# One core, three layers: the list that orders all operations and names their engines, made anew

## The chip, the cores and the metric

The kernel runs on one core of one Trainium2 chip. The core has TensorE (matmuls, PE in the rows), VectorE (DVE), ScalarE (ACT), GpSimd (POOL) and SyncE (SP), which here issues all transfers. Each engine works through its own queue in order; engines wait for each other by semaphores. The metric is the device time of one execution in microseconds (us), the median of the runs shown.

## What is computed

The reference chains three layers over 2 sequences of 768 tokens: a retention attention with 8 heads of 64 (blocks of 64 tokens, a decaying state of 64 x 64 for each head), a channel mix of width 512 with a hidden layer of 1024, and a gated convolution of five taps between two products of 512 x 512.

```python
intra = np.einsum('bhic,bhjc->bhij', qb, kb) * Dmask[None]
intra = np.einsum('bhij,bhjd->bhid', intra, vb)
inter = np.einsum('bhid,bhde->bhie', qb * lam_pow[None], kv_state)
out[:, :, sl] = intra + inter
...
xk = mu_k * x + (1.0 - mu_k) * x_prev
xr = mu_r * x + (1.0 - mu_r) * x_prev
k = np.maximum(xk @ w_k, 0.0)
v = k * k @ w_v
r = 1.0 / (1.0 + np.exp(-(xr @ w_r)))
x = (r * v)
...
gate_pre += conv_w[k][None, None, :] * xp[:, k:k + S, :]
gate = 1.0 / (1.0 + np.exp(-gate_pre))
return gate * (x @ w_val) @ w_out
```

`w_k`, `w_v`, `w_r`, `w_val`, `w_out` and `conv_w` come as float64; the kernel turns them into float32 itself, by work on their two 32-bit words.

## The kernel before

The program is a set of named operations, each of one or a few instructions, with a list of engines that may run it. A string, `ORDER`, lists all names in the order in which they are emitted, with a letter behind a colon where an operation may run on more than one engine (V VectorE, A ScalarE, G GpSimd); without a letter the first engine allowed is taken. `emit` walks the string. Each engine's queue is thus the string's operations of that engine, in the string's order; nothing else moves them. A name may stand only behind all that it depends on.

```python
    def emit(token):
        name, _, e = token.partition(":")
        o = ops[name]
        o.engine = e or o.engines[0]
        assert o.engine in o.engines and name not in emitted, token
        assert emitted.issuperset(o.deps), (token, o.deps - emitted)
        ...
        o.fn(of_letter[o.engine])
```

The names that the text uses, with their lines:

- *Weights* (`conversion`, L326 to L346), for each of 28 pieces of 128 x 512 that come from HBM: `a`, `b` on ScalarE; `c` (L331), `d`, `e` (L337), `f` (L340) on VectorE, `c` and `f` on GpSimd also; then the split of the float32 into a high part `h` (ScalarE) and a low part `l` (L346, VectorE or GpSimd). Every product is made of three matmuls, high by high, high by low and low by high, so that each operand, weights and activations alike, has a high and a low part.
- *Attention*, twelve chunks c of 128 tokens: transposes `Tk`, `Tq` on TensorE and their copies `Ek`, `Eq`; query times decay powers `Q` (L488); key times decay `D` (L497); scores `S` (L513), their product with the mask `M` (L520, VectorE, scores in PSUM); state products `U` (L534); state times decay `O` (L553) and the sum `N` (L556); output `Y`, `Z` (L595), copied to SBUF by `X` (L622, L624).
- *Channel mix*, six groups g of 256 tokens: `mk`, `mr` are the two mixes: a scaling `a0`, `a1` (L647, L649; any of three engines), a scaled sum `b0`, `b1` (L652, VectorE), the high part `h` and the low part `l` (L632). `r` is the sigmoid branch, `k` the hidden layer (relu `e`, square into the high part `h`, square again `q` (L749, L751), low part `l` (L757)), `v` the product back and its multiplication with r (L767), into tile `big` (`x2`).
- *Gated convolution*, for each g and each half m: the gate `g` in two pieces, a first tap as a scaling (L801, L803) and four more taps as scaled sums (L799, VectorE alone), then a sigmoid (L808); the split of x2 `s` (L777, L779); the value product `a` with its multiplication by the gate (L818) and its split (L632); the last projection `p` (L836), its copy (L843, L844) and the output transfer.
- `warm0` to `warm23` (L903): products of the identity that no one reads; ten of them stand at the end.

TensorE's products land in four PSUM tiles that are used in turn, the activations in rings of 26 tiles of 512 and 8 of 1024 floats, and the raw weights of the last layer in a ring of three.

Of the kernel before, what the change touches and what calls it, by code (L numbers as in the profile page):

```python
# [27 lines left out]
    Eq3:A w3f:G w1 Y2 N2.1 Z2 U3 S3 Q3 w0h mr0.0h mr0.0l:G w0l:G mr0.1a1:A q4 O3.0:V N3.0 X2:A
    M3 mr0.1b1 mr0.1b0 w3h w1a Tk4 Ek4:A w1c:V D4:G O3.1:G w1d v4 w3l:V mr0.1h w1e Y3 Z3 X3:A
    r0.1.0 mk0.0b1 Tq4 mk1.0a0:A r0.0.0 N3.1 mk0.1a1:V mk1.1a1:G w1b mr1.0a0:A mr1.1a0:A  # L30
    mr1.0a1:A mk1.0b0 Eq4:A w1f:V w1h k5 mr1.0b0 mk0.1b1 Tk5 mr1.0b1 mr1.1b0 mr1.1a1:A mr1.1b1
    mr0.1l:G w1l:G U4 mr1.0h w6 S4 Ek5:A O4.0:V w6a r0.1.1 mr1.0l:V mr1.1h x0 w6b r0.0.1 r0.0s
    r1.0.0 r0.1s mk1.0a1:G mk0.0a0:V jk3.1 w6c:V w6d w4 mk0.0b0 w7 mr1.1l:G w6e mk1.0b1 N4.0
    r1.0.1 w6f:G O4.1:V N4.1 r1.1.0 v5 mk0.0h mk1.1a0:G M4 D5:G w4a w4c:V q5 Tq5 w4d mk0.0l:G
    w7a Q4 w4e mk0.1a0:A mk0.1b0 w6h w6l:G w7c:V w4b w4f:V r1.1.1 Y4 w7d U5 mk1.0h Z4 H2 w7b
    w5 w5a w5c:V w5d Eq5:A w5b mk1.1b0 w4h jq3.2 mk1.0l:G w4l:G r1.1s S5 k0.1.0 r1.0s w9
    k1.1.0 w10 w10a mk0.1h w7e w5e w8 w7f:V w8a Q5 w8b w7h w10c:V k0.0.0 w9a mk1.1b1 mk1.1h
    jq3.3 jq3.0 w9b w5f:G w16 w16b w10d w5h w7l:V mk0.1l:G k1.0.0 mk1.1l:G w8c:V w8d w8e
    k0.1.1 w9c:V k1.1.1 w9d jk3.3 w8f:V w11 w5l:G w16a jq3.1 w9e w12 w11a k1.0.1 w11c:V jk3.0
    k7 M5 w8h w11b w8l:V k1.0e:A w9f:G O5.0:G w9h k1.1e:A w9l:G w10b k0.1e:A w11d w12a k0.0.1  # L40
    w12c:G w17 N5.0 w10e jk3.2 w10f:V X4:A k0.2.0 k1.1h k1.2.0 k1.2.1 k0.0e:A Bq3 w11e w11f:G
    k6 v6 Bk3 w12b w10h w10l:G k0.2.1 w15 D6:V Y5 jq4.1 Q6:G k1.0h k1.0q:A w13 S6 w16c:V w17a
    U6 w11h w11l:G Z5 jq4.0 w12d k0.3.0 k1.3.0 X5:A v7 w16d k1.3.1 w16e w16f:V w16h D7:G
    k1.0l:V jq4.2 w17b M6 w17c:V k0.0h N6.0:V O6.1:G w12e w12f:G w17d w16l:G N6.1 k0.3.1 w13a
    U7 k0.1h k0.2e:A k1.2e:A Q7:G w17e w17f:V k0.0q:A mr2.0a0:G v8 Y6 w12h S7 k0.1q:G k0.1l:G
    Z6 k0.0l:V w15a w14 w17h w12l:V v0.1.0 w17l:V v1.0.0 w15c:V jq4.3 k1.1q:A k1.1l:V w13c:V
    mk2.0a0:A w13b w14a k0.3e:A v1.1.0 k0.2h w13d w13e v1.1.1 k1.3e:A M7 w15d O7.0:G w14c:V
    w13f:V w13h w13l:G w15e v0.0.0 w14d jk4.3 w15b mk2.0b0 k8 w14b w18 w15f:V mk2.0a1:A N7.0
    D8:G k0.2q:A mk2.1a1:V mk2.0b1 mk2.1b1 v0.1.1 v1.0.1 O7.1:G w15h X6:V N7.1 w14e w14f:V
    k1.2h Y7 U8 k0.2l:G k1.3h w18a w14h w15l:V mr2.1a0:A Z7 w14l:V k11 jk4.1 k1.3q:A w18c:V  # L50
    w18d w18e w18b w18f:V H3 mk2.1a0:A k0.3h v0.0.1 mk2.1b0 k1.2q:G jk4.0 k1.2l:G v0.0.2
    v1.0.2 k0.3q:A k1.3l:G v1.0.3 k0.3l:V v0.0.3 w18h jk4.2 cw0 mk2.0h X7:A Bq4 v1.0e mk2.0l:G
    mk2.1h k2.0.0 mk2.1l:V k2.0.1 v9 Bk4 v0.0e S8 k9 k2.1.0 Q9:G k2.1.1 w19 w19a jk5.1 O8.0:G
    jk5.0 M8 k2.0e:V k2.3.0 w18l:G mk3.0a0:A k2.3.1 mk3.1a1:G mk3.1b1 mk3.0a1:V w19b D11:G
    k2.1e:V N8.0 mr3.0a0:G mr3.0b0 cw cwa D9:G cwb mr3.0a1:V Q8:V O8.1:G Y8 N8.1 mr2.0a1:A S9
    mk3.1a0:G mk3.1b0 mk3.0b0 Z8 U9 k2.3e:A O9.0:V N9.0 v0.1.2 jq5.0 k2.0h mr2.1b0 k2.2.0
    k2.0q:V jq5.1 k2.2.1 mk3.0b1 mk3.0h jk5.3 jq5.3 w19c:V w19d w19e w19f:V k2.2e:V w19h
    mr2.0b1 M9 v10 mk3.0l:G k3.1.0 k3.3.0 cwc:V w19l:G v1.1.2 jk5.2 v1.1.3 H4 mk3.1h mk3.1l:G
    mr2.1a1:V mr2.1b1 mr2.1h cwd k3.3.1 k10 k2.0l:V k3.1.1 X8:A mr2.1l:G mr2.0b0 mr2.0h Y9
    k2.1h O9.1:V Bk5 D10:V N9.1 jq5.2 Bq5 U10 k2.3h k2.3q:A k2.3l:V S10 Z9 X9:V v1.1e  # L60
    mk4.0a1:A s0.0h v0.1.3 M10 Q10:V v0.1e mr2.0l:G mk4.1a1:V mk4.1b1 k2.2h k2.2q:A O10.0:V
    cwe cwf:V k3.2.0 k3.2.1 N10.0 mr3.1a1:A O10.1:V v11 mk4.1a0:A mk4.1b0 k2.2l:G N10.1
    k3.2e:A mk4.1h cwg r2.0.0 mr4.1a1:G cwt r2.0.1 k3.1e:V k3.1h S11 Y10 mk4.0a0:V Q11:G
    mr3.1a0:G U11 g0.1.10:A Z10 O11.0:V X10:A r2.1.0 r2.0s mk4.0b0 r2.1.1 k2.1q:A H5 mr4.0a1:G
    M11 N11.0 Y11 Z11 k3.0.0 g1.1.10:V k3.1q:G k3.1l:V v2.0.0 r2.1s mr3.1b1 x1 mr4.0a0:A
    mr4.1a0:G k2.1l:G mr4.1b0 mr4.0b0 k3.3e:A X11:A mr5.1a1:V mk5.1a1:V mr3.1b0 mr3.0b1 v2.1.0
    mr4.0b1 mr3.0h v2.0.1 mk4.1l:G k3.2h mr5.0a1:A v2.0.2 v2.0.3 mk5.0a1:V mk4.0b1 k3.2q:G
    mk4.0h v2.0e s2.0h mk4.0l:G g2.0.00:A mk5.1a0:V k4.2.0 k4.2.1 mk5.1b1 mk5.1b0 mk5.1h
    k4.2e:V k4.3.0 k3.0.1 k3.0e:A k3.0h k3.0q:G k3.0l:V k4.1.0 k4.1.1 k4.1e:V g2.0.10:V
# [903 lines left out]
```

## Time and profile before

| | us |
|---|---|
| median of 3 runs | 347.18 |
| lowest and highest | 346.81, 349.31 |
| the profiled execution | 347.84 |
| its span, first to last instruction | 346.1 |
| VectorE busy, taps of the gates alone | 276.9, 62.5 |
| TensorE busy | 303.9 |
| mean granted TensorE clock | 0.951 |

An engine's busy time counts the union of its instructions. Busy matmuls overlap by their pipeline, so TensorE's work is better read from the time in which many follow each other without a gap. A group's mean duration includes any time in which an instruction was held after it had started. A wait names what ended last before an instruction could start.

### The profile page before, as it was taken

How to read it: one execution, taken by the hardware profiler on the slowest of the kernel's cores; microseconds unless marked ns; L12 is line 12 of the kernel's file. 1: busy time of each engine (PE TensorE's matmuls, PEld its weight loads, DVE VectorE, ACT ScalarE, POOL GpSimd, SP SyncE). 2: the span in 40 equal slices, each digit the busy share in tenths (PEclk: the TensorE clock that was granted, in tenths of full speed). 3: DMA queues.
4: the chain of work that ended last, by engine and by line, in shares of the span. 5: the costliest groups of instructions: out<-in, count | busy, mean ns of one | idle time of the engine just before them, and what ended most of it. 6: DMA issues, size and time to landing. Idle time of an engine off the chain costs nothing.

```text
span 346.1 us, 8383 instructions
## 1 busy us (share of the span) xinstructions
PE 303.9 (88%) x3488; PEld 286.7 (83%) x3488; DVE 276.9 (80%) x430; ACT 151.7 (44%) x272; POOL 174.8 (51%) x153
## 2 busy tenths in 40 slices
...
DMA packets 66052, 29.41 MB, mean 85 GB/s; under 512 B 58306, under 2 KB 58334, under 8 KB 66014
## 3 DMA queue, kind: packets, MB, share of 16 engines
...
## 4 chain that ended last, share of the span: by engine, by line
DVE 47%; PE 34%; issue 7%; SPq 6%; DMA 4%; ACT 1%; POOL 1%; DVEq 0%; POOLq 0%
DVE b_g L799 13%; PE b_a L675 8%; PE b_v L675 8%; PE b_k L675 6%; PE b_p L836 5%; SPq L302 3%; PE b_r L675 2%; PE xx L595 2%; SPq L281 2%; DVE b_mk_1a L652 2%; PE b_warm L903 2%; DVE b_g L803 1%; DVE b_w L340 1%; DMA b_k<-in_k_dram 1%; DMA b_lam<-in_lam_dram 1%
## 5 line engine op out<-in xcount | busy, mean ns | idle before, releaser
L799 DVE SCALAR_TENSOR_TENSOR b_g<-big,cw,b_g 128x256 f32<-128x256 f32 x96 | 62.5, 679 | 1.2
L675 PE MATMUL b_k<-b_mk_0h,w_rk 128*128 128x256 f32 x192 | 37.9, 286 | 1.3 <-ACT b_k_0e L743 0.9
L675 PE MATMUL b_k<-b_mk_1h,w_rk 128*128 128x256 f32 x192 | 36.0, 278 | 0.9 <-DVE w_rk L346 0.8
L675 PEld LDWEIGHTS b_k<-b_mk_0h,w_rk 128*128 128x128 f32 x192 | 31.2, 193 | 2.4 <-ACT b_k_0e L743 1.1
L675 PEld LDWEIGHTS b_k<-b_mk_1h,w_rk 128*128 128x128 f32 x192 | 30.3, 188 | 1.3 <-DVE w_rk L346 1.0
L675 PE MATMUL b_k<-b_mk_0l,w_rk 128*128 128x256 f32 x96 | 27.0, 282 | 0.0
L675 PE MATMUL b_k<-b_mk_1l,w_rk 128*128 128x256 f32 x96 | 26.6, 277 | 0.0
L675 PE MATMUL b_v<-b_k_1h,w_v 128*128 128x256 f32 x144 | 19.6, 285 | 1.0 <-POOL w_v L346 0.9
L675 PE MATMUL b_r<-b_mr_0h,w_rk 128*128 128x256 f32 x96 | 20.5, 297 | 0.0
L675 PE MATMUL b_r<-b_mr_1h,w_rk 128*128 128x256 f32 x96 | 19.9, 293 | 0.3 <-POOL w_rk L346 0.3
L595 PE MATMUL xx<-b_Q,state 64*64 64x64 f32 x352 | 12.6, 255 | 8.5 <-DVE b_X L624 3.7
L675 PE MATMUL b_a<-b_s_0h,b_y1h 128*128 128x256 f32 x48 | 14.2, 296 | 6.5 <-ACT big L727 3.3
L808 ACT ACTIVATE b_g<-b_g 128x512 f32<-128x512 f32 x12 | 7.6, 631 | 27.3 <-DVE b_g L799 27.1
L675 PEld LDWEIGHTS b_v<-b_k_1h,w_v 128*128 128x128 f32 x144 | 18.2, 191 | 1.6 <-POOL w_v L346 1.1
L675 PE MATMUL b_v<-b_k_0h,w_v 128*128 128x256 f32 x144 | 18.8, 281 | 0.6 <-DVE b_k_0h L757 0.6
L632 POOL TENSOR_TENSOR b_a_0l<-b_a_0e,b_a_0h 128x512 fp32r<-128x512 f32 x5 | 7.4, 1472 | 23.7 <-ACT b_a_0h L630 19.0
L595 PEld LDWEIGHTS xx<-b_Q,state 64*64 64x64 f32 x352 | 9.2, 155 | 12.1 <-issue 4.5
L675 PE MATMUL b_r<-b_mr_0l,w_rk 128*128 128x256 f32 x48 | 14.3, 299 | 5.5 <-DVE b_mr_0l L632 5.5
L675 PE MATMUL b_v<-b_k_2h,w_v 128*128 128x256 f32 x144 | 18.9, 280 | 0.0
L675 PE MATMUL b_v<-b_k_3h,w_v 128*128 128x256 f32 x144 | 18.8, 280 | 0.0
L632 POOL TENSOR_TENSOR b_mr_1l<-b_mr_1a,b_mr_1h 128x512 fp32r<-128x512 f32 x6 | 8.8, 1468 | 19.8 <-ACT b_mr_1h L630 19.8
L675 PEld LDWEIGHTS b_k<-b_mk_0l,w_rk 128*128 128x128 f32 x96 | 18.5, 192 | 0.0
...
## 6 DMA issues: line engine op xcount, KB each, us to landing
...
```

The costliest lines, as they stand in the source:

```text
L281: e.dma_start(dst[:, 4 * i:4 * i + 4, :], src[b, i::2, rows, :].rearrange("h p d -> p h d"),)
L302: e.dma_start(dst[p0:p0 + 32, n, :].rearrange("p (t e) -> p t e", e=32), src[b, head(n, s), t0:t0 + G, 32 * db:32 * db + 32].rearrange("(t ...
L340: op(f"{key}f", "VG", lambda e: e.tensor_tensor(words(I32, 1), xt(I32), words(I32, 0), op=ALU.add), reads=[raw, low, x], writes=[high])
L595: last = e.matmul(x[half[b_], j, at, :], w, m, start=spots[i] not in spots[:i], stop=spots[i] not in spots[i + 1:],)
L632: op(f"{name}l", "VG", lambda e: e.tensor_tensor(r(lo()), src(), f32(hi()), op=ALU.subtract), reads=[src, hi], writes=[lo])
L652: e.scalar_tensor_tensor(two(full)[:, i, :], xs[g]()[:, 2 * h + i, 0:G], rest[:, m0:m0 + 1], two(full)[:, i, :], op0=ALU.mult, op1=ALU.add,)
L675: e.matmul(out_[:, i, :], a, b, start=first and i == kk == n == 0, stop=last and i == kk == 1 and n == 2,)
L799: e.scalar_tensor_tensor(t, src, w, t, op0=ALU.mult, op1=ALU.add)
L803: e.tensor_scalar_mul(t, src, w)
L808: op(f"g{g}.{m}s", "A", lambda e: e.activation(acc(), acc(), AF.Sigmoid), writes=[acc])
L836: e.matmul(ps(), x, w, start=(m == kk == i == 0), stop=(m == NM - 1 and kk == 1 and i == 2),)
L903: e.matmul(warm_ps()[:, 0:P], ident, ident, start=True, stop=True)
```

## The change

Nothing but the string `ORDER` differs; all 972 lines stay as long as they are, and every operation of the one string stands in the other once. Two lines of the difference:

```diff
-    eye warm11 warm1 warm3 warm8 eye2 w2 zero w2a warm6 H0 w2c:V mu0 warm5 q0 k0 table warm4
...
+    eye warm5 warm8 warm7 w0 warm20 eye2 warm9 zero mu0 warm15 lam table q0 k0 Tq0 pows w0a
```

Of the operations that have a choice, GpSimd has 128 of more than 0.6 us before and 74 now; VectorE's instructions go from 430 to 462, ScalarE's from 270 to 291 (table loads left out). TensorE has the same matmuls in another order, and SyncE the same transfers.

By kind, before and now: low parts of weights 20 on GpSimd and 8 on VectorE, now 6 and 22; low parts of mixes 17 and 7, now 7 and 17; low parts of the hidden layer 10 and 14, now 11 and 13; of x2 8 and 4, now 4 and 8; of the gated value 9 and 3, now 8 and 4; scalings of the mixes 13 on GpSimd, 14 on VectorE, 21 on ScalarE, now 6, 10, 32; first taps 5, 12, 7, now 7, 5, 12; second squares 9, 1, 14, now 1, 4, 19.

The first place is GpSimd's queue while the hidden layer of the first two groups runs. `mk` are mixes, `w_rk` low parts of weights, L340 the last step of a weight's conversion, L553 a state product. Before:

```order
L614 COPY b_H_899<-b_H_453 128x4
L632 TENSOR_TENSOR b_mk_0l<-b_mk_0a_629,b_mk_0h 128x512
L346 TENSOR_TENSOR w_rk<-big_75,w_rk 128x512
L340 TENSOR_TENSOR big_75<-b_w5a,big_75 128x512
L632 TENSOR_TENSOR b_mk_1l<-b_mk_1a_645,b_mk_1h 128x512
L632 TENSOR_TENSOR b_mk_1l<-b_mk_1a_647,b_mk_1h 128x512
L346 TENSOR_TENSOR w_rk<-big_75,w_rk 128x512
L340 TENSOR_TENSOR b_w_951<-b_w9a,b_w_951 128x512
L553 TENSOR_TENSOR state_66<-state_65,pw 128x256
```

Now, at the same place of the program:

```order
L346 TENSOR_TENSOR w_rk<-big_75,w_rk 128x512
L497 TENSOR_TENSOR b_k_559<-b_k_559,kdec 128x512
L553 TENSOR_TENSOR state_65<-state_64,pw 128x256
L346 TENSOR_TENSOR w_rk<-b_w_844,w_rk 128x512
L340 TENSOR_TENSOR b_w_932<-b_w8a,b_w_932 128x512
L340 TENSOR_TENSOR b_w_827<-b_w9a,b_w_827 128x512
L553 TENSOR_TENSOR state_66<-state_65,pw 128x256
L497 TENSOR_TENSOR b_k_1221<-b_k_1221,kdec 128x512
```

The mixes' low parts (L632) are gone from it and stand in VectorE's queue instead; key decays (L497) and state products (L553) are left, with fewer operations between them.

The second is VectorE's queue while TensorE runs the products of groups 2 to 5 back to back. L799 is a tap of a gate, L652 and L632 belong to mixes, L757 to the hidden layer, L767 is the end of the `v` product. Before:

```order
L745 TENSOR_SCALAR b_k_1e<-b_k_1_0_2669 128x512
L803 TENSOR_SCALAR b_g_0_00_2604<-big_76,cw 128x256
L803 TENSOR_SCALAR b_g_1_10_2391<-big_76,cw 128x256
L757 TENSOR_TENSOR b_k_2h<-b_k_2e,b_k_2h 128x512
L649 TENSOR_SCALAR b_mk_0a_2593<-b_X_2419,mu 128x256
L652 SCALAR_TENSOR_TENSOR b_mr_1a_2333<-b_H_2119,rest,b_mr_1a_2333 128x256
L767 TENSOR_TENSOR big_76<-b_v_1_0_2535,big_76 128x2x256
L652 SCALAR_TENSOR_TENSOR b_mk_0a_2593<-b_X_2419,rest,b_mk_0a_2593 128x256
L799 SCALAR_TENSOR_TENSOR b_g_1_10_2391<-big_76,cw,b_g_1_10_2391 128x256
L652 SCALAR_TENSOR_TENSOR b_mk_0a_2593<-b_X_2419,rest,b_mk_0a_2593 128x256
L632 TENSOR_TENSOR b_mk_0l<-b_mk_0a_2593,b_mk_0h 128x512
L632 TENSOR_TENSOR b_mk_1l<-b_mk_1a_2531,b_mk_1h 128x512
```

Now:

```order
L632 TENSOR_TENSOR b_mr_0l<-b_mr_0a_2039,b_mr_0h 128x512
L799 SCALAR_TENSOR_TENSOR b_g_0_00_2619<-big_76,cw,b_g_0_00_2619 128x256
L767 TENSOR_TENSOR big_76<-b_v_0_0_2630,big_76 128x2x256
L751 TENSOR_TENSOR b_k_1e<-b_k_1e 128x512
L799 SCALAR_TENSOR_TENSOR b_g_1_00_2535<-big_76,cw,b_g_1_00_2535 128x256
L799 SCALAR_TENSOR_TENSOR b_g_0_00_2619<-big_76,cw,b_g_0_00_2619 128x256
L632 TENSOR_TENSOR b_mr_0l<-b_mr_0a_2418,b_mr_0h 128x512
L799 SCALAR_TENSOR_TENSOR b_g_0_10_2707<-big_76,cw,b_g_0_10_2707 128x256 x4
L757 TENSOR_TENSOR b_k_1h<-b_k_1e,b_k_1h 128x512
L652 SCALAR_TENSOR_TENSOR b_mr_0a_2864<-b_H_2316,rest,b_mr_0a_2864 128x256
L632 TENSOR_TENSOR b_mk_1l<-b_mk_1a_2624,b_mk_1h 128x512
L767 TENSOR_TENSOR big_76<-b_v_1_0_2645,big_76 128x2x256
```

Taps now stand between the parts of mixes and of the hidden layer; before, most of them stand further back in the queue.

The third is VectorE's queue about the fifth attention chunk, whose mask product is the row of L520. Before:

```order
L520 TENSOR_TENSOR b_M_814<-su,dmask 128x512
L331 TENSOR_SCALAR b_w4a<-b_w4a 128x512
L334 TENSOR_SCALAR b_w4a<-b_w4a 128x512
L488 TENSOR_TENSOR b_Q_833<-b_Tq_624,pw 128x512
L337 SCALAR_TENSOR_TENSOR b_w4a<-big_75,b_w4a 128x512
L652 SCALAR_TENSOR_TENSOR b_mk_1a_645<-b_H_107,rest,b_mk_1a_645 128x256
L331 TENSOR_SCALAR b_w7a<-b_w7a 128x512
L340 ISA big_75<-big_75,b_w4a 128x512x2
L334 TENSOR_SCALAR b_w7a<-b_w7a 128x512
```

Now:

```order
L632 TENSOR_TENSOR b_mr_1l<-b_mr_1a_622,b_mr_1h 128x512
L553 TENSOR_TENSOR state_64<-state_66,pw 128x256
L652 SCALAR_TENSOR_TENSOR b_mk_0a_624<-b_X_519,rest,b_mk_0a_624 128x256
L652 SCALAR_TENSOR_TENSOR b_mk_0a_580<-b_H_206,rest,b_mk_0a_580 128x256
L331 TENSOR_SCALAR b_w10a<-b_w10a 128x512
L520 TENSOR_TENSOR b_M_794<-su,dmask 128x512
L334 TENSOR_SCALAR b_w10a<-b_w10a 128x512
L632 TENSOR_TENSOR b_mk_0l<-b_mk_0a_624,b_mk_0h 128x512
L556 TENSOR_TENSOR state_64<-su,state_64 128x256
L346 TENSOR_TENSOR w_rk<-big_75,w_rk 128x512
L652 SCALAR_TENSOR_TENSOR b_mk_1a_802<-b_X_519,rest,b_mk_1a_802 128x256
L652 SCALAR_TENSOR_TENSOR b_mk_1a_564<-b_H_206,rest,b_mk_1a_564 128x256
```

Low parts of mixes and weights (L632, L346) now stand ahead of and behind the mask product and the state sum (L556), among the same conversion steps.

## Rows read from the trace of the kernel before

**Rows 1.** Page, part 1: busy us (share of the span) xinstructions of each engine.
```profile
PE 303.9 (88%) x3488; PEld 286.7 (83%) x3488; DVE 276.9 (80%) x430; ACT 151.7 (44%) x272; POOL 174.8 (51%) x153
```

**Rows 2.** Page, part 4: the chain that ended last, shares by engine.
```profile
DVE 47%; PE 34%; issue 7%; SPq 6%; DMA 4%; ACT 1%; POOL 1%; DVEq 0%; POOLq 0%
```

**Rows 3.** Chain in order of time, TensorE: start us, us, what, matmuls.
```profile
122.07 2.83 PE b_k L675 x24
...
148.26 0.69 PE su L513 x32
149.06 0.97 PE xx L595 x48
...
174.13 9.53 PE b_k L675 x84
...
327.07 13.64 PE b_p L836 x60
340.71 4.46 PE b_warm L903 x40
```

**Rows 4.** Windows, stages A to E: us, then busy us (xinstructions) of each engine.
```profile
core 0: us, PE busy (x) PEld busy (x) DVE busy (x) ACT busy (x) POOL busy (x), PEclk, DMA share, GB/s
0.00:123.40 123.40, 98.30 (x1553) 90.87 (x1554) 107.79 (x160) 73.85 (x133) 79.27 (x80) 0.92 0.67 161
123.40:169.90 46.50, 44.09 (x755) 41.95 (x754) 41.21 (x75) 17.50 (x35) 27.29 (x26) 1.00 0.24 45
169.90:220.30 50.40, 50.40 (x438) 50.34 (x438) 28.23 (x41) 21.16 (x39) 20.07 (x16) 1.00 0.11 40
220.30:314.00 93.70, 79.94 (x555) 75.74 (x554) 85.48 (x133) 31.40 (x54) 42.64 (x30) 0.93 0.10 35
314.00:346.10 32.10, 31.17 (x197) 27.81 (x195) 14.23 (x24) 7.78 (x14) 5.58 (x4) 1.00 0.18 66
```

**Rows 5.** Windows of the same stages, VectorE instructions of line L799 alone.
```profile
core 0: us, DVE busy (x), PEclk, DMA share, GB/s
...
169.90:220.30 50.40, 4.04 (x6) 1.00 0.11 40
220.30:314.00 93.70, 51.53 (x77) 0.93 0.10 35
314.00:346.10 32.10, 6.89 (x13) 1.00 0.18 66
```

**Rows 6.** Waits of TensorE: who waited for whom, us, times, longest.
```profile
PE b_r L675 <- DVE b_mr_0l L632: 5.5, 2, 5.2
...
PE xx L595 <- DVE b_X L624: 3.7, 1, 3.7
PE b_a L675 <- ACT big L727: 3.3, 1, 3.3
PE b_a L675 <- DVE b_p_0e L844: 3.2, 1, 3.2
PE xx L595 <- DVE b_Q L488: 2.9, 1, 2.9
PE su L534 <- DVE state L556: 2.7, 1, 2.7
...
PE b_Tk L456 <- DMA b_k<-in_k_dram: 0.4, 1, 0.4
```

**Rows 7.** One line's instructions, VectorE: duration ns min/median/max, first and last start.
```profile
L799 DVE SCALAR_TENSOR_TENSOR b_g<-big,cw,b_g x96: 471/483/1542, 189.4 to 325.5; 128x256 f32<-128x256 f32 x96
...
L520 DVE TENSOR_TENSOR b_M<-su,dmask x12: 674/682/690, 13.5 to 161.4; 128x512 f32<-128x512 f32 x12
```

**Rows 8.** Timeline, 244 to 262 us, VectorE, then GpSimd: start us, us, what.
```profile
243.78 0.68 DVE L779 TENSOR_TENSOR b_s_0l<-big,b_s_0h 128x512 fp32r<-128x512 f32 x1
244.38 0.68 DVE L767 TENSOR_TENSOR big<-b_v,big 128x512 f32<-128x512 f32 x1
244.98 0.68 DVE L337 SCALAR_TENSOR_TENSOR b_y2a<-b_y,b_y2a 128x512 int32<-128x512 int32 x1
...
246.30 1.67 DVE L799 SCALAR_TENSOR_TENSOR b_g<-big,cw,b_g 128x256 f32<-128x256 f32 x4
...
248.67 0.35 DVE L803 TENSOR_SCALAR b_g<-big,cw 128x256 f32<-128x256 f32 x1
249.05 11.76 DVE L799 SCALAR_TENSOR_TENSOR b_g<-big,cw,b_g 128x256 f32<-128x256 f32 x13
...
248.88 1.32 POOL L346 TENSOR_TENSOR b_y2l<-b_y,b_y2h 128x512 fp32r<-128x512 f32 x1 [9.31 <-ACT b_y2h L344]
250.17 1.49 POOL L340 TENSOR_TENSOR b_y<-b_y3a,b_y 128x512 int32<-128x512 int32 x1
252.45 1.57 POOL L346 TENSOR_TENSOR b_y2l<-b_y,b_y2h 128x512 fp32r<-128x512 f32 x1 [0.79 <-ACT b_y2h L344]
253.99 1.47 POOL L779 TENSOR_TENSOR b_s_0l<-big,b_s_0h 128x512 fp32r<-128x512 f32 x1
255.43 1.46 POOL L779 TENSOR_TENSOR b_s_1l<-big,b_s_1h 128x512 fp32r<-128x512 f32 x1
256.85 1.45 POOL L779 TENSOR_TENSOR b_s_0l<-big,b_s_0h 128x512 fp32r<-128x512 f32 x1
```

**Rows 9.** Groups by line, VectorE's taps, then GpSimd: xcount | busy us, mean ns | idle.
```profile
L799 DVE SCALAR_TENSOR_TENSOR b_g<-big,cw,b_g 128x256 f32<-128x256 f32 x96 | 62.5, 679 | 1.2
...
L553 POOL TENSOR_TENSOR state<-state,pw 128x256 f32<-128x256 f32 x11 | 9.1, 827 | 8.4 <-DVE state L556 3.5 <-DVE state L550 3.3 <-DMA b_k<-in_k_dram 1.7
...
L632 POOL TENSOR_TENSOR b_mr_1l<-b_mr_1a,b_mr_1h 128x512 fp32r<-128x512 f32 x6 | 8.8, 1468 | 19.8 <-ACT b_mr_1h L630 19.8
...
L346 POOL TENSOR_TENSOR w_rk<-big,w_rk 128x512 fp32r<-128x512 f32 x5 | 7.2, 1448 | 3.9 <-ACT w_rk L344 3.9
...
L751 POOL TENSOR_TENSOR b_k_2e<-b_k_2e 128x512 f32<-128x512 f32 x3 | 3.4, 1142 | 9.4 <-ACT b_k_2h L754 9.4
```

**Rows 10.** Groups by line, ScalarE: a square and a scaling.
```profile
L749 ACT ACTIVATE b_k_3e<-b_k_3e 128x512 f32<-128x512 f32 x4 | 2.5, 628 | 0.1
...
L647 ACT ACTIVATE b_mr_1a<-b_H,mu 128x256 f32<-128x256 f32 x5 | 2.5, 495 | 0.0
```

More of the change, by code (lines that the diff above doesn't have):

```diff
@@ L28 @@
[L28 to L69, printed above, removed]
@@ new lines @@
+    w12l:V Y6 w17e k1.2.1 H3 k1.1h k0.2e:A w16b w13a w16f:V mk2.0a0:A w13c:V w17f:V w13d
+    k0.3e:A w16h Z6 w17h w16l:V w14 w13e w17l:V jq4.0 w13f:V k10 w14a U7 k1.2e:A k8 jq4.3
+    w14c:V w14d Q7:V k1.1q:A k1.2h w15 O7.0:V jq4.2 w13h k1.1l:V w13l:V k0.3h k0.0l:G X6:A
+    N7.0 w14e w14b O7.1:V N7.1 mk2.1a0:A v1.0.0 M7 k1.2q:A w15a w15c:V v0.0.0 v0.1.0 w14f:V
+    k0.1l:G v0.1.1 D8:V jq4.1 v1.1.0 v1.1.1 k0.3q:A k0.2h Y7 mr2.1a1:A w15b v1.0.1 mr2.1a0:G
+    v0.0.1 Z7 v8 w14h w15d w14l:V k1.3h w15e mk2.0a1:G k0.2q:A w15f:V jk4.0 k0.2l:V k0.3l:V k9
```

120 lines of the change are left out of this document (78 added, 42 removed).

## The prediction

> **What bounds the kernel now.** I first read the busy shares: TensorE 303.9 us and VectorE 276.9 us of 346.1, GpSimd 174.8, ScalarE 151.7 [rows 1]. The chain that ended last gives VectorE 47% and TensorE 34% [rows 2]. So neither engine bounds it all; they take turns. To see where, I cut the program at places that exist in both orders: where TensorE has done 80, 120, 170 and 240 us of its work. Its work is priced at full clock from rows: 84 matmuls of 128x256 in 9.53 us, 0.113 us each; 60 of the last projection in 13.64, 0.227 each; 40 warming ones in 4.46; an attention step some 2 to 3 us by its parts [rows 3]. That makes 271 us in both orders. In the order before, the cuts fall at 123.4, 169.9, 220.3 and 314.0 us, and I call the stages A to E [rows 4]:
>
> - A, 123.4 us: VectorE busy 107.8 and idle 15.6, mostly at the start; TensorE did 80.7 us of work. VectorE bounds.
> - B, 46.5: TensorE busy 44.1, VectorE 41.2. Shared.
> - C, 50.4: TensorE busy all of it, VectorE 28.2. TensorE bounds.
> - D, 93.7: VectorE busy 85.5, TensorE 79.9 at a granted clock of 0.93, for 70.6 us of work. VectorE bounds.
> - E, 32.1: TensorE busy 31.2. TensorE bounds.
>
> The fault to see: VectorE has 22 us of nothing in C and is the brake in D. In D stand 77 of the 96 convolution taps, and they took 51.53 us, 0.67 each [rows 5]. TensorE waits there in pieces: 5.2 us for a low part, 3.3 and 3.2 at the value product [rows 6].
>
> **What a GpSimd operation costs VectorE.** The shortest tap took 471 ns, the median 483, the longest 1542 [rows 7]. Between 249.05 and 260.81 thirteen taps took 11.76 us beside six GpSimd operations that ran nearly without a gap; four taps just before took 1.67 us, so 0.40 from start to start [rows 8]. Thirteen at 0.40 are 5.2: 6.5 us are stall, 1.09 for each of the six. The mask product, with one operand in PSUM, never stalled: 674 to 690 ns [rows 7]. The Trainium skill, "SBUF — State Buffer", section "Who interferes with whom", says that the two engines share a port pair as an exclusive lock, and that a VectorE instruction with two SBUF inputs contends where one with a single SBUF input does not; the trace agrees, by these two rows.
>
> For all of VectorE I take each instruction at the shortest duration of its kind, less the 0.08 us by which neighbours overlap (0.68 us long, 0.60 from start to start [rows 8]). That gives 188 us for the 430 instructions; busy is 277, so 89 us are stall. GpSimd runs 128 operations of more than 0.6 us: 0.70 us of stall each. By stage: A 37.4 us for 58 (0.64), B 10.4 for 22 (0.47), C 9.5 for 15 (0.63), D 28.6 for 29 (0.99), E 3.1 for 4 (0.78).
>
> **The change, part by part.** All operations stay; their engines and their order change. *GpSimd* loses 54 of 128: low parts of splits 28 fewer, scalings 5, squares 8, the rest decays, conversions and state products. They cost it 0.8 to 1.5 us each [rows 9]. *ScalarE* gains 21, net: 11 scalings and 5 first taps at 0.50, 5 squares at 0.63, little else: 11 us on an engine busy for 44%, hidden in its idle time [rows 1, 10]; without that cover it would be these 11 us. *VectorE* gains 32, net: 28 low parts, 4 conversion ends, 3 squares, 3 decays, 3 query products at 0.60 (0.56 for a decay), a few of the smaller ones, less 11 scalings and first taps at 0.26 (0.35 long, 0.27 without the overlap [rows 8]). Sum +22.7 us, so 210.6. Against it go 54 stalls of 0.70, 38 us. VectorE as a whole: 277 - 38 + 23 = 262. A low part that moves from GpSimd to VectorE saves 0.70 and costs 0.60: nearly nothing; the gain is in those that go to ScalarE, and in the order.
>
> The order is the larger part. Free VectorE work (base) by stage, before by the order of its queue and after: A 68.6 and 82.4; B 31.6 and 30.5; C 21.7 and 36.7; D 53.3 and 44.5; E 12.7 and 16.5. Large GpSimd operations after: 29, 10, 12, 17, 6. Taps go from 11 to 31 in C, and from 71 to 41 in D. So, with the stall per operation of each stage:
>
> - A: 82.4 + 29 x 0.64 = 101.0, and 15.6 idle as before: 116.6, **-6.8**.
> - B: VectorE 30.5 + 10 x 0.47 = 35.2, no longer the limit; TensorE's busy 44.1 stays as 44: **-2.5**.
> - C: VectorE 36.7 + 12 x 0.63 = 44.3 under TensorE's 50.4, which stays the limit; 1 us for the lost slack: **+1**.
> - D: VectorE 44.5 + 17 x 0.99 = 61.3. TensorE's 70.6 us of work at the pace of C (50.4 for 49.3) are 72.2. Of the 13.8 us in which it now idles I keep half: 79, **-14.7**. Keeping none or all gives 72 and 86, the two ends.
> - E: VectorE 16.5 + 6 x 0.78 = 21.2 under TensorE's 30.3; the last taps stand later: **+1.5**. The end itself (last projection, output, ten warming products) is of the same length.
>
> Sum -21.5: a span of 324.6. The profiled execution took 347.84 for its span of 346.1, and stands 0.66 over the median of 347.18; so 324.6 + 1.74 - 0.66 = 326 us. SyncE issues the same transfers, the decay factors and first weights sooner. I cost that at nothing: TensorE's waits for a transfer come to 0.4 us [rows 6], and A's transfers fill 0.67 of its time [rows 4], so they would fit in 83 us; only a stage A under that would be held by them.
>
> The stall of an operation is the unknown price: its ends are 0.47 (stage B) and 1.09 (the six operations above). I take each stage's own, since the kinds that meet there stay the same.
>
> **Rivals.** *1, the stall grows and nothing is won (347).* VectorE idles less, so each GpSimd operation that is left meets it more often. At 1.09 everywhere: A 82.4 + 31.6 + 15.6 = 129.6 (+6.2), B 41.4, about TensorE's pace (+0.5), C 49.8 against 50.4, so hand-offs of 3.6, D at 63 of VectorE keeps more of its waits, 82 (-11.7), E +1.5. Sum 0.1. For it: D has 0.99 already. Against: A, with VectorE busy for 107.8 of its 123.4 us, has 0.64. And the mean of 0.70 over all 128 says that most operations meet VectorE only in part. The Trainium skill, "SBUF — State Buffer", "Who interferes with whom", has the loser of the lock wait for the whole instruction of the other; taken for every operation, that comes to this rival's 347.
>
> *2, attention waits behind the converted weights (358).* In A and B the queue of VectorE holds many more low parts (21 of weights and mixes, where 8 stood in A), in order, ahead of the mask products, state sums and query products on which TensorE's attention steps wait. Such a wait now costs 3.7, 2.9 and 2.7 us where it shows [rows 6]. At 2.7 more for each of the 12 steps: +32, against -21.5 a loss of 11. It turns to a loss from 1.8 us a step on. Against it: by VectorE's queue with stalls, the seventh and eighth step (the ones on whose results the second half of A rests) come some 5 and 9 us earlier than before, since 26 and 28 large GpSimd operations fewer stand ahead.
>
> *3, both engines run level (313).* D at 72.2 (-21.5), B at 41 (-5.5), A -6.8, no loss in C and E: -33.8. For it: no stage would be bound by VectorE after A. Against: two engines at 80 to 100% that exchange data in order hardly do it without waits, as B shows now.
>
> **How the numbers follow.** Forecast 0.62 (its own range 317 to 337), rival 1 0.14, rival 2 0.14, rival 3 0.10. A measurement of this kernel tells about 1% from no change: faster is the forecast and rival 3, 0.72; within 1% is rival 1, 0.14; slower is rival 2, 0.14. Range 313 to 349: it reaches to rivals 3 and 1 and leaves out the slower case, and a little at both ends.
>
> **What would show it.** VectorE's busy time near 262 us, with a mean tap clearly under the 679 ns of now [rows 9]; GpSimd near 104. The first hidden-layer unit of group 2 on TensorE near 117 us in place of 122 [rows 3]. TensorE without its waits of 5.2, 3.3 and 3.2 us in the gate stage, and VectorE busy by over 80% in C. Wrong is the forecast if TensorE's waits for VectorE in attention grow past 20 us in total (rival 2), or if stall per GpSimd operation is near 1.1 (rival 1).

## The result and the profile after

The changed kernel takes 313.73 us, the median of four runs (312.80 to 316.74), where before takes 347.0, the median of four; the ratio is 0.904, with a 95% interval of 0.897 to 0.912. The profiled execution has a span of 312.5 us, 33.6 less than before [rows 4]. The forecast was 326 us in a range of 313 to 349: the kernel is faster, as forecast, but by 33 us in place of 21, at the lower edge of the range, outside the 317 to 337 of the forecast alone, and at the number of rival 3. The ratios of the later kernels compare fast runs of one session, so they can differ by up to 0.7% from the quotients of the medians in the table.

The page of after, parts 1 and 4, answers to [rows 1, 2]:

```profile
PE 296.9 (95%) x3488; PEld 281.5 (90%) x3488; DVE 256.8 (82%) x462; ACT 157.8 (50%) x292; POOL 104.0 (33%) x100
...
PE 77%; DVE 6%; ACT 1%; issue 1%; DVEq 0%
```

VectorE has 32 instructions more and is busy for 20 us less; GpSimd fell from 174.8 to 104.0. The chain that ended last was VectorE's for 47% and is now TensorE's for 77%. By the chain, TensorE now bounds the kernel.

The windows of after, cut where TensorE has done the same work as at the cuts of [rows 4], stages A to E (columns as there):

```profile
0.00:108.20 108.20, 95.97 (x1557) 88.90 (x1557) 95.60 (x179) 71.67 (x133) 44.60 (x52) 0.94 0.77 180
108.20:150.80 42.60, 42.18 (x742) 40.32 (x741) 35.81 (x71) 22.42 (x44) 13.91 (x16) 1.00 0.28 57
150.80:206.90 56.10, 54.37 (x450) 54.16 (x447) 44.36 (x78) 24.02 (x47) 13.59 (x11) 0.97 0.09 30
206.90:280.70 73.80, 73.46 (x560) 70.57 (x560) 63.22 (x105) 32.66 (x58) 26.69 (x20) 1.00 0.13 44
280.70:312.50 31.80, 30.95 (x191) 27.59 (x189) 17.79 (x32) 7.04 (x12) 5.26 (x4) 1.00 0.22 82
```

| stage | before | forecast | after | off by |
|---|---|---|---|---|
| A | 123.4 | 116.6 | 108.2 | -8.4 |
| B | 46.5 | 44 | 42.6 | -1.4 |
| C | 50.4 | 51.4 | 56.1 | +4.7 |
| D | 93.7 | 79 | 73.8 | -5.2 |
| E | 32.1 | 33.6 | 31.8 | -1.8 |

In D TensorE is busy for 73.46 of 73.80 us. Its waits of 5.2, 3.3 and 3.2 us [rows 6] are gone; the largest that are left (who waited for whom: us, times, longest) lie elsewhere:

```profile
PE su L513 <- ACT b_Eq L459: 3.9, 1, 3.9
PE b_r L675 <- DVE b_mr_1l L632: 1.7, 1, 1.7
PE su L534 <- DMA b_v<-in_v_dram: 1.4, 1, 1.4
```

The taps of the gates as a group, and their windows of C and D (us, VectorE busy, clock, DMA share, GB/s), answer to [rows 9, 5]:

```profile
L799 DVE SCALAR_TENSOR_TENSOR b_g<-big,cw,b_g 128x256 f32<-128x256 f32 x96 | 54.9, 598 | 3.7 <-ACT b_g L801 2.9
```

```profile
150.80:206.90 56.10, 16.56 (x28) 0.97 0.09 30
206.90:280.70 73.80, 26.88 (x49) 1.00 0.13 44
```

22 more taps stand in C, 28 fewer in D, and the mean of one fell from 679 to 598 ns. By the same reckoning as before the change (each instruction at the shortest of its kind), VectorE's free work is 210.4 us and its stall 46.3: 0.63 for each of the 74 large GpSimd operations. Some 15 us of it are left by this reckoning in a kernel whose GpSimd runs no large operation (below), so 0.63 is an upper figure.

C is the one stage that lost. Its first wait shows why. VectorE, then GpSimd, then TensorE, in the timeline of after (start us, us, what):

```profile
151.64 1.11 DVE L649 TENSOR_SCALAR b_mr_1a<-b_H,mu 128x256 f32<-128x256 f32 x1
...
153.68 1.53 DVE L751 TENSOR_TENSOR b_k_0e<-b_k_0e 128x512 f32<-128x512 f32 x1
155.13 1.51 DVE L799 SCALAR_TENSOR_TENSOR b_g<-big,cw,b_g 128x256 f32<-128x256 f32 x1
...
157.82 0.68 DVE L632 TENSOR_TENSOR b_mr_1l<-b_mr_1a,b_mr_1h 128x512 fp32r<-128x512 f32 x1
...
151.30 1.30 POOL L757 TENSOR_TENSOR b_k_3h<-b_k_3e,b_k_3h 128x512 fp32r<-128x512 f32 x1
...
153.51 1.15 POOL L751 TENSOR_TENSOR b_k_2e<-b_k_2e 128x512 f32<-128x512 f32 x1
154.74 1.61 POOL L757 TENSOR_TENSOR b_k_2h<-b_k_2e,b_k_2h 128x512 fp32r<-128x512 f32 x1
...
158.55 0.39 PE L675 MATMUL b_r<-b_mr_1l,w_rk 128*128 128x256 f32 x1 [1.74 <-DVE b_mr_1l L632]
```

A scaling, a square and a tap, which take 0.34, 0.68 and 0.48 us at their shortest, take 1.11, 1.53 and 1.51 beside GpSimd's low parts and its square. That is 2.65 us of stall ahead of the low part of a mix, and TensorE waits 1.74 us for it.

### The profile page after: what moved, and what is told of

Same layout as the page of the kernel before. It is cut to its first block, busy times and chain, and to the rows that moved or that the text cites. A ratio compares the mean times of both kernels' runs of the same rounds, so it can differ in the third digit from the quotient of the medians.

```text
span 312.5 us, 8376 instructions
## 1 busy us (share of the span) xinstructions
PE 296.9 (95%) x3488; PEld 281.5 (90%) x3488; DVE 256.8 (82%) x462; ACT 157.8 (50%) x292; POOL 104.0 (33%) x100
## 4 chain that ended last, share of the span: by engine, by line
PE 77%; DVE 6%; ACT 1%; issue 1%; DVEq 0%
PE b_v L675 22%; PE b_k L675 21%; PE b_a L675 11%; PE b_p L836 9%; PE b_r L675 7%; PE xx L595 3%; PE b_warm L903 1%; DVE b_g L799 1%; PE su L513 1%; PE su L534 1%; DVE b_mk_0a L652 1%; DVE b_s_0l L779 0%; DVE b_k_0e L751 0%; DVE b_mr_1l L632 0%; DVE b_w10a L331 0%
## 5 line engine op out<-in xcount | busy, mean ns | idle before, releaser
L799 DVE SCALAR_TENSOR_TENSOR b_g<-big,cw,b_g 128x256 f32<-128x256 f32 x96 | 54.9, 598 | 3.7 <-ACT b_g L801 2.9
L675 PE MATMUL b_k<-b_mk_1h,w_rk 128*128 128x256 f32 x192 | 37.5, 282 | 0.0
L675 PE MATMUL b_r<-b_mr_0h,w_rk 128*128 128x256 f32 x96 | 18.9, 283 | 0.5 <-ACT b_Eq L459 0.5
L675 PEld LDWEIGHTS b_v<-b_k_0h,w_v 128*128 128x128 f32 x144 | 18.7, 199 | 0.1
L675 PE MATMUL b_v<-b_k_3h,w_v 128*128 128x256 f32 x144 | 18.7, 280 | 0.0
L675 PEld LDWEIGHTS b_k<-b_mk_1l,w_rk 128*128 128x128 f32 x96 | 18.1, 189 | 0.2
L675 PEld LDWEIGHTS b_v<-b_k_2h,w_v 128*128 128x128 f32 x144 | 17.8, 188 | 0.2
L675 PEld LDWEIGHTS b_v<-b_k_3h,w_v 128*128 128x128 f32 x144 | 17.7, 188 | 0.1
L632 POOL TENSOR_TENSOR b_a_0l<-b_a_0e,b_a_0h 128x512 fp32r<-128x512 f32 x5 | 6.5, 1309 | 31.1 <-DVE b_a_1l L632 13.9
L903 PE MATMUL b_warm<-ident 128*128 128x128 f32 x96 | 15.6, 324 | 1.3 <-POOL ident masks.py:199 1.3
L675 PEld LDWEIGHTS b_r<-b_mr_0h,w_rk 128*128 128x128 f32 x96 | 15.5, 189 | 0.7 <-ACT b_Eq L459 0.7
```

What stands on the lines that cost most here:

```text
L632: op(f"{name}l", "VG", lambda e: e.tensor_tensor(r(lo()), src(), f32(hi()), op=ALU.subtract), reads=[src, hi], writes=[lo])
L675: e.matmul(out_[:, i, :], a, b, start=first and i == kk == n == 0, stop=last and i == kk == 1 and n == 2,)
L799: e.scalar_tensor_tensor(t, src, w, t, op0=ALU.mult, op1=ALU.add)
L903: e.matmul(warm_ps()[:, 0:P], ident, ident, start=True, stop=True)
```

## The experiments

The theory was the forecast's: a large GpSimd operation costs VectorE 0.5 to 1.1 us, the letters and the order each pay a part, and the parts add up. Stages are cut by TensorE's work as above.

| kernel | us | A | B | C | D | E |
|---|---|---|---|---|---|---|
| before | 347.0 | 123.4 | 46.5 | 50.4 | 93.7 | 32.1 |
| after | 313.7 | 108.2 | 42.6 | 56.1 | 73.8 | 31.8 |
| order of before, engines of after | 338.1 | 118.1 | 46.7 | 52.4 | 84.6 | 34.1 |
| order of after, engines of before | 354.7 | 143.9 | 47.2 | 54.7 | 75.9 | 33.6 |
| ten weight parts back | 334.9 | 131.0 | 42.1 | 56.1 | 73.9 | 31.8 |
| GpSimd empty | 333.7 | 132.2 | 43.8 | 51.4 | 73.3 | 31.9 |
| GpSimd empty, earlier places | 310.7 | 106.2 | 43.9 | 51.4 | 73.4 | 31.8 |
| 24 readers in D | 322.0 | 110.4 | 42.4 | 56.2 | 81.2 | 32.1 |
| 24 x 3 writers in D | 317.7 | 109.9 | 42.5 | 54.5 | 78.2 | 31.9 |
| 24 x 2 writers in D | 312.7 | 108.0 | 42.4 | 53.6 | 73.7 | 31.8 |
| GpSimd empty from C on | 309.8 | 107.2 | 42.3 | 51.4 | 73.4 | 31.8 |
| the same, no products at the end | 307.9 | 108.3 | 42.5 | 51.4 | 73.4 | 30.1 |

The stages are those of one profiled execution, the times medians of two to five runs. Kernels that have after's A, or its C, still differ there by some 3 us (A 107.2 to 110.4, C 53.6 to 56.2), so no smaller difference in these two is read.

### The letters alone, and the order alone

164 names differ in their letter. The first kernel has before's order and after's letters, the second the reverse.

```diff
 first, against before        second, against after
-... w2l:G ... w11l:G ...     -... w2l:V ... w11l:V ...
+... w2l:V ... w11l:V ...     +... w2l:G ... w11l:G ...
```

> The order of before with the engines of after. The theory (what a GpSimd operation costs VectorE and the order each pay a part; stall per operation by stage 0.5 to 1.0 us): VectorE's free work by stage is 82.0, 32.5, 25.7, 57.2, 13.3 us beside 27, 13, 9, 21 and 4 large GpSimd operations; A 112, B 44, C 50.4, D 86, E 32, so a span of 324 and 326 us. Rival 'the order does it all': 347 (no gain). Rival 'the engines do it all': 314. In each case GpSimd's busy time near 104 us and VectorE's stalls near 50 us.

> The order of after with the engines of before. The theory: free VectorE work by stage 69.7, 28.2, 33.7, 39.5, 16.8 us beside 57, 18, 22, 27 and 4 large GpSimd operations; A 120, B 43, C 56, D 75, E 32: 326 to 328 us. Rival 'the order does it all': 314. Rival 'the engines do it all': 347. GpSimd's busy time near 175 us, stalls near 80 us.

Measured: 338.1 us (ratio to before 0.981, 0.965 to 0.997) and 354.7 us (1.029, 1.006 to 1.052). Both were forecast near 326. The letters alone bring 7 to 10 us and the order alone loses 7 to 10, by the ratios and by the medians; neither interval lies wholly more than 2% from before. The two together bring 33. The parts do not add up; theory and both rivals miss. Windows A and D of the first kernel, then of the second:

```profile
0.00:118.10 118.10, 97.19 (x1554) 90.55 (x1555) 102.66 (x184) 74.91 (x137) 42.05 (x52) 0.91 0.72 169
...
217.20:301.80 84.60, 76.00 (x554) 71.48 (x553) 76.44 (x130) 33.63 (x61) 29.19 (x21) 0.98 0.11 38
```

```profile
0.00:143.90 143.90, 106.18 (x1558) 98.95 (x1559) 104.83 (x156) 69.97 (x128) 77.91 (x80) 0.83 0.58 136
...
245.80:321.70 75.90, 74.00 (x560) 70.51 (x559) 64.58 (x95) 31.48 (x56) 38.91 (x28) 1.00 0.13 43
```

In D the order alone reaches 75.9 us, near after's 73.8 (the theory said 75), with nearly before's load on GpSimd. So the order is what freed D: 46 of the taps are left in it where before has 77, and 7 other operations of VectorE have left it too. The letters alone bring it to 84.6 (said 86). The taps in D of the second kernel (us, VectorE busy, clock, DMA share, GB/s):

```profile
245.80:321.70 75.90, 32.98 (x46) 1.00 0.13 43
```

In A the order alone is 20 us worse than before, and 36 worse than after. VectorE is busy there for 104.83 of 143.90 us: it is not short of time. TensorE waits for GpSimd (waits of the second kernel):

```profile
PE b_r L674 <- POOL w_rk L345: 8.7, 2, 4.6
PE b_k L674 <- POOL w_rk L345: 8.7, 1, 8.7
PE b_v L674 <- DVE b_k_0h L756: 5.1, 1, 5.1
```

### Ten low parts of weights

The waits name low parts of weights, so the ten of stage A whose letter changed were put back, in after's order.

```diff
-w2l:V w4l:V w6l:V w9l:V w10l:V w11l:V w13l:V w16l:V w3l:G w7l:G
+w2l:G w4l:G w6l:G w9l:G w10l:G w11l:G w13l:G w16l:G w3l:V w7l:V
```

> After, with the ten low parts of weights in stage A that changed engine put back where before has them: eight go to GpSimd again, two to VectorE; the order and all else stay. With all of before's engines in after's order stage A took 143.9 us in place of 108.2, and TensorE waited 17.4 us there for low parts of weights on GpSimd. Theory 'these ten carry that loss': waits for them of over 10 us again, A 123 to 140, time 328 to 345. Rival 'the mixes' parts and the squares that went back with them made GpSimd late': A under 115, time 314 to 320.

Measured: 334.9 us (0.9625, 0.953 to 0.972), with A at 131.0 and B to E as in after. Ten letters of 164 carry 22.8 of the 35.7 us by which the second kernel's A is longer than after's; the other 12.9 were not followed up. The new theory is one of queues. The first product of the sigmoid branch needs `w0l`, which stands some 75 names behind the one that VectorE is at when GpSimd runs it. In after GpSimd's queue is short, and `w0l` is the first row here (GpSimd, timeline of after; three parts, `w0l`, `w3l`, `w1l`):

```profile
27.64 1.55 POOL L346 TENSOR_TENSOR w_rk<-big,w_rk 128x512 fp32r<-128x512 f32 x1
...
30.23 1.30 POOL L346 TENSOR_TENSOR w_rk<-big,w_rk 128x512 fp32r<-128x512 f32 x1
33.21 1.30 POOL L346 TENSOR_TENSOR w_rk<-big,w_rk 128x512 fp32r<-128x512 f32 x1 [1.67 <-ACT w_rk L344]
```

VectorE reaches that place of the list at 48.7 us in after's trace: GpSimd ran 21 us ahead of it. With `w2l` put back, `w2l` stands in front and waits for its own high part, with `w0l` behind it (the kernel with ten parts back, GpSimd; the row holds two instructions, `w2l` and then `w0l`):

```profile
41.24 2.72 POOL L345 TENSOR_TENSOR w_rk<-big,w_rk 128x512 fp32r<-128x512 f32 x2 [11.56 <-ACT w_rk L343]
```

GpSimd sat idle for 11.56 us with work behind the waiting instruction, `w0l` ended at 43.96 in place of 29.19, and TensorE waited 4.7 us for a low part there, and 5.5 and 6.1 for two of GpSimd's results later on.

### GpSimd emptied, and the places mended

If a letter only set the cost of an operation, emptying GpSimd would be free. Every operation that has a choice is taken off it (61 to VectorE, 14 scalings, first taps and squares to ScalarE; 25 small instructions without a choice, 5.8 us, stay); the second kernel moves twenty of those in A forward as well, to where VectorE stood when GpSimd ran them in after.

```diff
 GpSimd empty                     the places mended
-... mk1.0b1 w0l:G r0.0.0 ...    -... mr0.0b0 w1d ... mk1.0b1 w0l:V r0.0.0 ...
+... mk1.0b1 w0l:V r0.0.0 ...    +... mr0.0b0 w0l:V w1d ... mk1.0b1 r0.0.0 ...
```

> After, with every operation that has a choice taken off GpSimd: the scalings, squares and first taps go to ScalarE, all others to VectorE. The theory (a GpSimd operation costs VectorE about as much as it saves it): VectorE's free work grows from 210 to about 243 us, its stalls fall from 46 to under 3, so its busy time falls by some 10 us, and the taps take 0.48 us each; the time is 309 to 316, like after (313.7), since TensorE bounds most of it. Rival 'VectorE needs the help': its busy time goes up, stages A and D grow, over 320 us.

> The kernel with GpSimd empty throughout, and twenty of the operations of stage A that it took off GpSimd moved forward in the list, to where VectorE stood when GpSimd ran them in after's trace (low parts of the first weights by some 75 places, second low parts of the hidden layer by 80). GpSimd ran these 3 to 21 us before VectorE reached their places in the list. Theory 'it was their place, not VectorE's load': A falls from 132.2 to 109 to 114 (VectorE's free work there is 94.2, stalls 4, idle 12 to 15 as in after), B to E as with GpSimd empty (200.4), so a span of 309 to 315, a time of 311 to 316. Rival 'VectorE cannot carry this work in A': A stays over 125, time over 327.

Measured: 333.7 us (0.967, 0.956 to 0.979), and 310.7 us (0.894, 0.8875 to 0.900) with the places mended. The first refutes what I expected, and its rival too: VectorE's busy time in A rose only from 95.60 to 98.34 us, and it is idle for 33.9. Over the whole kernel VectorE is busy for 257.8 us, where after has 256.8 and I expected some 10 less (page of the kernel with GpSimd empty):

```profile
PE 302.0 (91%) x3488; PEld 285.9 (86%) x3488; DVE 257.8 (78%) x523; ACT 163.9 (49%) x306; POOL 5.8 (2%) x25
```

Against some 243 us of free work, the expectation's figure, that leaves 15 us that no large operation of GpSimd can have caused. By this difference about 31 of after's 46.3 us of stall are GpSimd's, an estimate of 0.43 us an operation. In load the exchange is nearly even, as the theory said. Window A, the wait and the instruction behind it (same kernel):

```profile
0.00:132.20 132.20, 103.69 (x1558) 96.03 (x1559) 98.34 (x204) 73.65 (x137) 5.01 (x23) 0.86 0.63 148
```

```profile
PE b_r L674 <- DVE w_rk L345: 7.8, 1, 7.8
```

```profile
47.24 0.69 DVE L345 TENSOR_TENSOR w_rk<-big,w_rk 128x512 fp32r<-128x512 f32 x1
```

That row is `w0l`: the same operation, half as long as on GpSimd, and it ends 18.7 us later. With its place mended it runs on VectorE at 26.71, and A falls by 26 us with the same engines and the same operations. Window A and the rows of `w0l` and `w3l` (kernel with places mended):

```profile
0.00:106.20 106.20, 94.10 (x1558) 87.78 (x1559) 97.45 (x204) 72.96 (x136) 6.75 (x23) 0.95 0.78 183
```

```profile
26.71 0.68 DVE L345 TENSOR_TENSOR w_rk<-big,w_rk 128x512 fp32r<-128x512 f32 x1
...
28.37 0.68 DVE L345 TENSOR_TENSOR w_rk<-big,w_rk 128x512 fp32r<-128x512 f32 x1
```

So it was their place. GpSimd's worth in A is not that it takes work off VectorE but that its queue lets late-listed work run early; without it, the list must say so itself.

### What holds VectorE up

24 instructions are put on GpSimd in stage D that nothing waits for: products of the mask with itself, or fills of it with zeros, after its last use.

```diff
+    def pad(e):
+        e.tensor_tensor(dmask, dmask, dmask, op=ALU.mult)   # readers
+        # writers: e.memset(dmask, 0.0), three times or twice
+    for i in range(24):
+        op(f"pad{i}", "G", pad, reads=[], writes=[mask_b])
```

> After, with 24 more GpSimd operations spread over stage D, each a product of the mask with itself in place, 128x512, after the mask's last use (the output isn't touched by it). The theory (a GpSimd operation with SBUF inputs holds up VectorE by 0.5 to 1.1 us): VectorE gets 12 to 26 us more to do in D, 63 to 75 to 89, passes TensorE's 73 us; D grows by 5 to 14 us, the time to 319 to 328, and the mean tap rises from 598 to over 650 ns. Rival 'GpSimd's operations do not hold up VectorE, only their order counts': under 2 us, taps unchanged.

> After, with GpSimd kept about as busy in stage D as by the 24 readers of the run before, at the same 24 places, but by operations that only write: each place fills the 128x512 mask three times with zeros, after its last use (the output isn't touched by it). The readers cost VectorE 15.0 us of stall in D (0.63 each), 7.3 us of D's length and 8.2 us of the time, 322. Theory 'the two engines collide over what they read': here stalls in D stay within 3 us of after's 14.4, D stays 74 to 76, time 313 to 316, mean tap near 598 ns. Rival 'any work of GpSimd in SBUF holds VectorE up, or its queue is late': as with the readers, 320 or more.

> As the run with writers, with two fills of the mask in place of three at each of the 24 places (some 26 us of GpSimd; the readers took 29.8, the three fills 39.2). Stage D was 73.8 without, 78.3 with three fills at an unchanged stall of 15.2, and 81.1 with the readers. Theory 'the three fills only made GpSimd's own queue late': with less work than the readers D comes back to 74 to 76, the stall stays near 15, time 314 to 316. Rival 'operations on GpSimd that only write slow the kernel as readers do': D 77 or more, time 318 or more.

Measured: 322.0 us (0.934, 0.913 to 0.955), 317.7 (0.913, 0.906 to 0.921) and 312.7 (0.899, 0.890 to 0.908). Window D and the groups of taps and of the added instructions, of the kernel with readers, then with 24 x 2 writers:

```profile
209.00:290.20 81.20, 75.99 (x561) 72.12 (x560) 77.89 (x105) 32.82 (x58) 57.14 (x44) 0.98 0.12 40
```

```profile
L800 DVE SCALAR_TENSOR_TENSOR b_g<-big,cw,b_g 128x256 f32<-128x256 f32 x96 | 63.6, 688 | 3.7 <-ACT b_g L802 2.9
...
L932 POOL TENSOR_TENSOR dmask<-dmask 128x512 f32<-128x512 f32 x24 | 29.8, 1240 | 0.8
```

```profile
204.00:277.70 73.70, 73.36 (x561) 70.47 (x560) 65.29 (x105) 32.98 (x58) 52.28 (x68) 1.00 0.13 45
```

```profile
L800 DVE SCALAR_TENSOR_TENSOR b_g<-big,cw,b_g 128x256 f32<-128x256 f32 x96 | 57.3, 623 | 3.7 <-ACT b_g L802 2.9
...
L933 POOL MEMSET dmask<- 128x512 f32 x48 | 26.4, 550 | 2.0
```

The readers add 15.0 us of stall to D's 14.4, 0.63 each; VectorE is then busy for 77.89 of 81.20 us and sets the stage again. TensorE's waits in that D are all for VectorE, the longest of them:

```profile
PE b_r L676 <- DVE big L768: 2.5, 1, 2.5
```

26.4 us of writing, close to the readers' 29.8, add some 2 us of stall, and D stays as in after. With three fills the stall stayed too (15.2), but D grew by 4.4 us, more than I expected: GpSimd was busy for 64 of 78 us there, and its own queue was late. VectorE waited for it longest at a step of a weight's conversion, 4.6 us, where it waited 1.2 with two fills and not at all with the readers (kernel with three fills):

```profile
DVE b_z0a L335 <- POOL b_z0a L332: 4.6, 1, 4.6
```

The Trainium skill, "SBUF — State Buffer", section "Who interferes with whom", says that a VectorE instruction with two SBUF inputs contends with a GpSimd instruction that reads SBUF and not with one that only writes it; these two kernels agree, by 15.0 us of added stall against 2.

### Cleared where VectorE is crowded

From C on nothing seemed to need GpSimd's lead, and its stalls cost C its wait. So after's A and B stay, and GpSimd is empty from C on (26 operations to VectorE, 9 to ScalarE). In a second kernel the ten products of the identity that run last are left out.

```diff
-... g0.1.10:G ... k2.2l:G ... mk5.0l:G ...
+... g0.1.10:A ... k2.2l:V ... mk5.0l:V ...
 and in the second:
-    for i in range(WARM):
+    for i in sorted(set(range(WARM)) - {1, 3, 6, 10, 11, 13, 14, 18, 22, 23}):
```

> After, with GpSimd cleared of every operation that has a choice from stage C on alone (scalings, first taps and squares to ScalarE, the rest to VectorE); A and B as in after. Theory (in A the GpSimd queue holds operations that would block VectorE's queue, from C on it only takes VectorE's time): A and B 150.8 as in after, C 51.4, D 73.3, E 31.8 as with GpSimd empty throughout; span 307.3, time 308.5. Rival 'stage C's loss has another cause' (its higher number of taps, or mixes on ScalarE): C stays near 56, time 312 to 315. Rival 'VectorE needs the help in C and D': over 316.

> The kernel with GpSimd cleared from stage C on, without the ten products of the identity at the end, which no one reads (they are left out). In after they run from 307.19 to 311.65 us, while the last output tile is copied by 307.9 and its transfer takes some 2 us. Theory: the span then ends with that transfer, 1.5 to 2 us sooner than with the products: 306.5 to 307. Rival 'the end waits for the transfer anyway': no difference.

Measured: 309.8 us (0.8915, 0.886 to 0.897) and 307.9 us (0.883, 0.877 to 0.889). Windows C and D of the first:

```profile
149.50:200.90 51.40, 51.40 (x446) 51.40 (x447) 43.04 (x89) 25.25 (x50) 0.00 (x0) 1.00 0.10 33
200.90:274.30 73.40, 73.40 (x561) 70.50 (x560) 59.37 (x116) 34.48 (x62) 0.00 (x0) 1.00 0.12 44
```

TensorE is busy for all of C and D. VectorE has 11 instructions more in C, is busy for 1.3 us less, and the wait of 1.74 us is gone: C's loss was stall, as the first theory has it. The interval of the ratio only just touches after's; that of the second kernel lies below it, and it is the fastest here, by 11.7% against before. The 1.7 us from E are the part that leaving the products out was to give; by the times alone the two kernels are not told apart (307.9 to 310.8 and 304.6 to 308.3).

The copy of the fourth chunk's query, for which TensorE waited 3.6 to 3.9 us, was then put one place ahead, before the query product that held it.

```diff
-... Tq3 Q3 w2 w1h Eq3:A S3 ...
+... Tq3 Eq3:A Q3 w2 w1h S3 ...
```

> The fastest kernel so far (GpSimd cleared from stage C on, no products of the identity at the end, 307.9) with one operation moved by one place: the copy of the fourth chunk's transposed query to SBUF (ScalarE) now stands ahead of the query product that reads the same PSUM tile (VectorE), as it does for the third chunk. In that kernel the copy started at 36.47, 2.62 us after ScalarE was free, released by the query product, and TensorE waited 3.62 us for it before the scores at 37.12. Theory: the copy runs at 33.5, the scores start near 34.3, TensorE's wait goes; VectorE, which is busy there, gains only its own wait of 0.85 us for the scores, so A is 0.9 to 3 us shorter, time 305 to 307. Rival 'VectorE sets the pace there': A within 0.5 us of 108.3, time 307.5 to 308.5.

Measured: 307.5 us (304.2 to 308.9, five runs; 0.892, 0.883 to 0.900), the same as without it. In its profile, of the shortest of those runs, the scores start at 33.02 in place of 37.12 and the wait is 1.77, by the profile for a mix's high part; A is 105.3 there. Whether A is shorter in the other runs the times do not tell: no verdict.

## Why the forecast was right, and where it was off

- **What bounds what.** Right for C and D: D was VectorE's, C had its slack, and the taps went from D into C. D gave 19.9 of the 33.6 us, A 15.2. "VectorE bounds" is not shown for A: VectorE is busy there for 95 to 108 us in the kernels whose A is shown, while A takes 106.2 to 143.9. By places alone it changed by 26 us.
- **The stall of a GpSimd operation.** Right in kind. By the forecast's own reckoning it is 0.63 in after where 0.70 was forecast, and the added readers cost 0.63; but that reckoning counts some 15 us that are not GpSimd's, without which after has about 0.43. VectorE's busy time is 256.8 where 262 was forecast, GpSimd's 104.0 as said. Rival 1 (1.09 everywhere) is out.
- **D, the term that was mis-sized by 5.2.** The step "of the 13.8 us in which it now idles I keep half" failed: 0.3 us were kept. With VectorE at 63.22 us, ten below TensorE's 73.46, nothing waits; with 76.44 (letters alone) or 77.89 (readers) D is 84.6 or 81.2. The floor of 72.2 was good to 1.3 us. VectorE's own sum in D was good (63.22 against 61.3). The objection raised against rival 3, that two busy engines hardly run level, did not hold for engines at 86% and 100%. Rival 3 has the total right by some luck: it put A at -6.8 and C at none, measured are -15.2 and +5.7, and these two errors partly cancel.
- **A, mis-sized by 8.4.** Its three terms were all too high: free work 80.8 against 82.4, stall 14.8 against 18.6 (0.51 an operation, not before's 0.64), idle 12.6 against 15.6. "Idle as before" had no ground: it is 12.6 in after, 33.9 with GpSimd empty, 8.7 with places mended. Why the stall of one fell in A was not tried.
- **C, mis-sized by 4.7 the other way.** I took 1 us "for the lost slack". VectorE's sum there was right (44.36 us against 44.3), by less free work and more stall, 0.99 an operation in place of 0.63. What failed is that a sum under TensorE's leaves TensorE the limit: the stall came where a mix was due. The clock granted to TensorE was 0.86 between 160 and 170 us, behind the wait. In the two kernels with writers, which have the same operations in C and the same wait, the clock stayed at 1.00 and C was 54.5 and 53.6, so some 2 us of the loss, an estimate, are the clock's. With GpSimd empty C is 51.4, my number. The stretch of after, and C with 24 x 2 writers:

```profile
160.00:170.00 10.00, 10.00 (x77) 10.00 (x76) 3.90 (x10) 4.75 (x10) 0.00 (x0) 0.86 0.07 27
...
150.40:204.00 53.60, 51.89 (x446) 51.68 (x447) 43.66 (x78) 23.93 (x47) 12.64 (x11) 1.00 0.10 31
```

- **B and E** were off by 1.4 and 1.8 us, both too high; the 1.5 us for taps that stand later in E did not show.
- **The step that was wrong in kind** is "a low part that moves from GpSimd to VectorE saves 0.70 and costs 0.60: nearly nothing". In load that is so. But I took letter and order as two terms of one sum, and the experiments' expectations of 326 for each alone failed by 12 and 28 us. A letter also says when an operation runs: ten low parts of weights are worth 21 us by that. The forecast's direction came out because after's letters and order fit each other; the load alone could not have told that, so this much of it is luck.
- **Rival 2** named the wrong victim: attention did not wait behind the converted weights (TensorE's waits for VectorE in scores and state products come to 1.1 us), but its fear, work late in an in-order queue, is what the order with before's letters shows, for the weights themselves.
- **What would show it.** Group 2's first hidden unit came at 106.80 where 117 was forecast; C's VectorE share is 79% (over 80 was said).
